# A weight transposed by TensorE in place of a DMA transpose, and another weight loaded from ScalarE's queue

## The chip, the cores and the metric

The kernel runs on one core of a Trainium2 chip. The metric is the device time of one execution in microseconds (us), measured around the whole program. The five engines of a core that matter here are PE (TensorE, the matrix unit), DVE (VectorE), ACT (ScalarE), POOL (GpSimd) and SP (SyncE, which here only issues transfers). Each takes its own instructions strictly in order, so an instruction that waits holds up everything behind it on its engine. Transfers are issued from SP, ACT or POOL and are carried by sixteen DMA engines that all of them share.

## What is computed

The reference is a transformer block with its gradient. The forward part is a pre-norm attention over a short dilated window (each token sees itself and seven earlier tokens, two apart, 32 heads of width 16), followed by a pre-norm feed-forward layer with the tanh form of gelu. Sizes: 2048 tokens, width 512, hidden width 1792, all in bf16.

```python
h  = x + attention(layernorm(x), wqkv) @ wo     # window of 8 tokens, stride 2
u  = layernorm(h) @ w1 + b1                     # [2048, 1792]
h2 = h + gelu(u) @ w2 + b2                      # first output
```

The other seven outputs are the gradients of `sum(h2 * grad_out)` with respect to x, wqkv, wo, w1, b1, w2 and b2. For the change it matters that the backward pass needs `w2` transposed: the gradient of the gelu output is `grad_out @ w2.T`.

## The kernel before

The 2048 tokens are worked on in four chunks of 512 (`NC = 4`, `CH = 512`). In a name such as `psq2_10` of the code the first digit is the chunk. Activations mostly go with tokens on the 128 partitions, or transposed with features on the partitions.

The forward pass goes through these functions, each called once for a chunk `c`. `f_ln1` normalises and transposes the input. `f_qkv(c, sel)` multiplies by one third of `wqkv` and writes the result to scratch tensors in device memory (`q_r`, `k_r`, `v_r`), from where it is read back in another layout. `f_attn` makes the logits (products on DVE, line 313, whose sums over the head width PE does with a matrix of ones, `sel`, line 320), the softmax (the exponential is line 436), and writes the weights to the scratch tensor `at_r` from POOL (line 179). `f_o` reads them back into the tile `a` (line 300, four small transfers on SP), multiplies them with `v` on DVE (line 330, tiles `pbo`), sums on PE (line 336, `pso`), copies the sums on ACT (line 451, `otm`) and transposes the result (lines 274 and 276, `pto` and `oT`). `f_h` multiplies by `wo` (line 463, `psh`), adds the input, normalises and transposes again (`ptb`, `ln2T`). `f_ffn1` is the first feed-forward product (line 506, `psf`) and gelu, which uses ACT (lines 508, 510, 518) and DVE (515, 516, 520) in turn. `f_ffn2` is the second product (line 535, `ps`) and needs `w2` as it lies in memory.

The functions are Python that emits instructions. `mix` and `take` interleave two generators by hand: `mix(f_ffn1(2), f_ffn2(1))` lets the second product of one chunk fill the first of the next. After that a scheduler places the instructions of each engine with its own estimate of when operands are ready, so the order on an engine differs from the order of the source. `gate(ins, key)` makes an instruction wait until a marked one has run: `("e", 1, 0)` is the first exponential of chunk 1, `("e", 3, 1)` the second of chunk 3, `("o", 1, 0)` the first `otm` copy of chunk 1.

PSUM tiles are taken by tag. `ptile(name, "T")` and `ptile(name, "U")` each have one buffer: 128 partitions times 1024 bf16 elements, which holds eight transposed blocks of 128 by 128. A second set of eight can start only when the first has been copied out. The tags "A", "B" and "L" have two buffers.

Weights: `w1` is loaded once as it lies, by POOL, into the slot of tag "w1", which the tiles for x of chunks 1 and 2 and the transposed ln1 of chunk 1 used before. `w2` is loaded likewise. The backward pass needs `w2T` and `w1T`; both are made by a DMA transpose on SP that reads the weight from device memory (lines 602 and 632). `w2T` takes the slot of `wqkv`, whose own transposes (`turn_w_gen`, lines 483 to 495) are made by PE before. Its first reader is the backward product at line 697 (`psg`). On SP's queue the transpose stands directly ahead of the four loads of `a` for chunk 3.

The backward pass runs over the chunks in the order 3, 0, 1, 2, first through the feed-forward layer (`b1_gg`, `b1_gx`, with `gw2_gen` between), then through attention.

Of the kernel before, what the change touches and what calls it, by code (L numbers as in the profile page):

```python
# [10 lines left out]
P = 128  # L11
BF16 = mybir.dt.bfloat16
# [23 lines left out]
def kernel(  # L36
# [20 lines left out]
    nc = tc.nc  # L57
# [5 lines left out]
    F = B_w1.shape[1]  # L63
# [3 lines left out]
    DC = D // P  # L67
    FT = F // P
# [8 lines left out]
    def pool(name, bufs, side="left", space=None):  # L77
        kw = {} if space is None else {"space": space}
        return tc.alloc_tile_pool(name=name, bufs=bufs, side=side, reuse_waits="tile", **kw)
# [15 lines left out]
    def acc(name, tag="A"):  # L95
        return psum.tile([P, CH], F32, name=name, tag=tag, bufs=1 if tag in "TU" else 2)

    def ptile(name, tag="T"):
        return psum.tile([P, 8 * P], BF16, name=name, tag=tag, bufs=1 if tag in "TU" else 2)
# [4 lines left out]
    sync, pq = nc.sync, nc.gpsimd  # L104
    mark = {}

    def behind(ins, first):
        tc.add_manual_dep(ins.ins, first.ins.name,
                          mybir.DependencyInfo(mybir.DependencyClass.Sync, mybir.DependencyReason.DATA), reason="begin later")

    def gate(ins, key):
        behind(ins, mark[key])


    ident = const.tile([P, P], BF16, name="ident")
# [41 lines left out]
    def pv(d_t):  # L157
        return d_t[:, :].rearrange("p (t d) -> p t d", t=TC)
# [26 lines left out]
    fw = pool("fw", 1, side="right")  # L185
# [14 lines left out]
    xs, w1, w2 = {}, [], []  # L200
    early1 = fl.tile([P, DC * F], BF16, name="early1", tag="w1", bufs=1)

    def load_x(c, nm="x", eng2=None):
        if nm == "x" and c in (1, 2):
            t_ = early1[:, c * TC * D:(c + 1) * TC * D].rearrange("p (j d) -> p j d", j=TC)
        else:
            t_ = get(fr, [P, TC, D], BF16, f"{nm}{c}", "x", 2)
        for ins in rows(sync, xf, c, t_, False, eng2):
            if nm == "x" and c in (1, 2):
                gate(ins, ("r", 3))  # L210
            if nm == "xr":
                gate(ins, ("o", c, 0))
        return t_
# [40 lines left out]
    def layernorm(src, dst, rstd, c, nm):  # L254
        st = const.tile([P, TC, 6], F32, name=f"st{nm}{c}", tag=f"st{nm}", bufs=2)
        mv = const.tile([P, TC, 2], F32, name=f"mv{nm}{c}", tag=f"mv{nm}", bufs=2)
        ve = const.tile([P, TC], F32, name=f"ve{nm}{c}", tag=f"ve{nm}", bufs=2)
        for j in range(TC):
            nc.vector.bn_stats(out=st[:, j, :], in_=src[:, j, :])
            nc.vector.bn_aggr(out=mv[:, j, :], in_=st[:, j, :])  # L260
        nc.vector.tensor_scalar(out=ve[:], in0=mv[:, :, 1], scalar1=EPS, scalar2=None, op0=ALU.add)
        r = rstd[:, c * TC:(c + 1) * TC]
        mark["r", c] = nc.gpsimd.tensor_tensor(out=r, in0=ve[:], in1=half[:], op=ALU.pow)
        for j in range(TC):
            nc.vector.tensor_scalar(out=dst[:, j, :], in0=src[:, j, :], scalar1=mv[:, j, 0:1],
                                    scalar2=r[:, j:j + 1], op0=ALU.subtract, op1=ALU.mult)

    def to_T(src, dst, nm, tag, tag2=None):
        for d2 in range(DC // 2):
            pt = ptile(f"pt{nm}{d2}", tag2 if tag2 and d2 else tag)  # L270
            for i in range(2):
                for j in range(TC):
                    dc = 2 * d2 + i
                    nc.tensor.transpose(pt[:, (i * TC + j) * P:(i * TC + j + 1) * P],  # L274
                                        src[:, j, dc * P:(dc + 1) * P], ident[:])
            nc.scalar.copy(out=dst[:, 2 * d2:2 * d2 + 2, :], in_=pt[:].rearrange("p (i t) -> p i t", i=2))
# [180 lines left out]
    def f_h(c):  # L457
        x, oT = load_x(c, "xr"), oTs.pop(c)
        h = fb.tile([P, TC, D], BF16, name=f"h{c}", tag="h", bufs=2)
        for j in range(TC):  # L460
            ps = acc(f"psh{c}_{j}")
            for g in range(G):
                nc.tensor.matmul(ps[:], lhsT=oT[:, g, j * P:(j + 1) * P], rhs=wo[:, g, :], start=(g == 0), stop=(g == G - 1))
            nc.vector.tensor_tensor(out=h[:, j, :], in0=ps[:], in1=x[:, j, :], op=ALU.add)
        ln2 = fr.tile([P, TC, D], BF16, name=f"ln2_{c}", tag="t1", bufs=1)
        layernorm(h, ln2, rstd2, c, "b")
        pq.dma_start(out=pv(ln2_d[c]), in_=ln2[:])
        ln2T = fl.tile([P, DC, CH], BF16, name=f"ln2T{c}", tag="ln2T", bufs=2)
        to_T(ln2, ln2T, f"b{c}", "U")
        hs[c], l2T[c] = h, ln2T  # L470
# [4 lines left out]
    def dgelu(y, u, s, t):  # L475

        nc.vector.tensor_tensor(out=y[:], in0=y[:], in1=u[:], op=ALU.mult)
        nc.scalar.activation(out=t[:], in_=s[:], func=ACT.Identity, bias=one_t[:], scale=-1.0)
        nc.vector.tensor_tensor(out=y[:], in0=y[:], in1=t[:], op=ALU.mult)
        nc.vector.tensor_scalar(out=y[:], in0=y[:], scalar1=1.0, scalar2=None, op0=ALU.add)  # L480
        nc.vector.tensor_tensor(out=y[:], in0=y[:], in1=s[:], op=ALU.mult)

    def turn_w_gen():

        for src, col, d_t in [(wqkv, sel * D, wqkv_d[sel]) for sel in range(3)] + [(wo, 0, wo_d)]:
# [8 lines left out]
            pq.dma_start(out=d_t[:, :], in_=t_[:].rearrange("p j d -> p (j d)"))  # L494
            yield

    def f_ffn1(c):
        ln2T = l2T[c]
        gts[c] = []
        for f2 in range(FT // 2):  # L500
            u = fl.tile([P, 2, CH], BF16, name=f"u{c}_{f2}", tag="u", bufs=3)
            for i in range(2):
                ft = 2 * f2 + i
                ps = acc(f"psf{c}_{ft}", "B")
                for dc in range(DC):
                    nc.tensor.matmul(ps[:], lhsT=w1[0][:, dc, ft * P:(ft + 1) * P], rhs=ln2T[:, dc, :],  # L506
                                     start=(dc == 0), stop=(dc == DC - 1))
                nc.scalar.activation(out=u[:, i, :], in_=ps[:], func=ACT.Identity, bias=b1c[:, ft:ft + 1], scale=1.0)  # L508
            z = fl.tile([P, 2, CH], BF16, name=f"z{c}_{f2}", tag="z", bufs=2)
            nc.scalar.activation(out=z[:], in_=u[:], func=ACT.Square)  # L510
            if c == 3:
                tag = "bu" if f2 < 4 else "bs"
                y = ys[f2] = br2.tile([P, 2, CH], BF16, name=f"y{c}_{f2}", tag=tag, bufs=4)
                nc.vector.tensor_scalar(out=y[:], in0=z[:], scalar1=6.0 * GC * GK, scalar2=2.0 * GC, op0=ALU.mult, op1=ALU.add)
            nc.vector.tensor_scalar(out=z[:], in0=z[:], scalar1=GK, scalar2=1.0, op0=ALU.mult, op1=ALU.add)
            nc.vector.tensor_tensor(out=z[:], in0=z[:], in1=u[:], op=ALU.mult)  # L516
            s = fl.tile([P, 2, CH], BF16, name=f"s{c}_{f2}", tag="s", bufs=2)
            nc.scalar.activation(out=s[:], in_=z[:], func=ACT.Sigmoid, scale=2.0 * GC)  # L518
            gt = fb.tile([P, 2, CH], BF16, name=f"g{c}_{f2}", tag="g", bufs=GB)
            nc.vector.tensor_tensor(out=gt[:], in0=u[:], in1=s[:], op=ALU.mult)  # L520
            gts[c].append(gt)
            if c == 3:
                dgelu(y, u, s, z)
            r0, r1 = 2 * f2 * P, (2 * f2 + 2) * P
            for dd, t_ in ((x_d[c][r0:r1, :], u), (s_d[c][r0:r1, :], s), (g_d[r0:r1, c * CH:(c + 1) * CH], gt))[2 if c == 3 else 0:]:
                pq.dma_start(out=dd.rearrange("(i p) t -> p i t", p=P), in_=t_[:])  # L526
            yield
# [14 lines left out]
    def take(gen, n=1):  # L542
        for _ in range(n):
            next(gen, None)

    def mix(gen, gen2, steps=1):
        for _ in gen:
            take(gen2, steps)
        take(gen2, 100)
# [30 lines left out]
    nc.vector.tensor_copy(out=b1c[:], in_=ptb[:, 0:FT])  # L580
    f_attn(1)
    w1.append(fl.tile([P, DC, F], BF16, name="w1", tag="w1", bufs=1))
    gate(pq.dma_start(out=w1[0][:], in_=B_w1.rearrange("(dc p) f -> p dc f", p=P)), ("e", 1, 0))
    f_o(0)
    f_h(0)
    f_qkv(2, 2)
    mix(f_ffn1(0), none)
    f_o(1)
    w2.append(fb.tile([P, FT, D], BF16, name="w2", tag="w2", bufs=1))
# [8 lines left out]
    f_h(2)  # L598
    take(turn_w, 2)
    f_attn(3)  # L600
    w2T = fw.tile([P, DC, F], BF16, name="w2T", tag="wq", bufs=1)
    gate(sync.dma_start_transpose(out=w2T[:], in_=B_w2[:, :]), ("e", 3, 1))
    mix(f_ffn1(2), f_ffn2(1))
    f_o(3)
    f_h(3)
    fr.release()
    br1 = pool("br1", 1, side="right")
    b1_order = (3, 0, 1, 2)
# [328 lines left out]
    for c in range(NC):  # L937
# [4 lines left out]
        if c == 2:  # L942
            load_otm()
            load_ln1a(bl, (0, 1, 2), ("g", 3, 0))
            for sel in range(3):
                gate(pq.dma_start(out=wqkvT[:, sel * DC:(sel + 1) * DC, :],
                                  in_=wqkv_d[sel][:, :].rearrange("p (j d) -> p j d", j=DC)), ("g", 3, 0))
# [12 lines left out]
    wg, wq, wk = gwqkv_gen(2), gwqkv_gen(0), gwqkv_gen(1)  # L960
# [54 lines left out]
```

## Time and profile before

| | before |
|---|---|
| median of 6 runs | 708.0 us (705.83 to 710.4) |
| the profiled execution, its own time | 710.08 us |
| its span from first to last instruction | 708.3 us |
| TensorE clock granted, mean | 0.96 |
| busy: PE, DVE, ACT, POOL | 89%, 78%, 56%, 30% |
| moved by DMA | 163.57 MB |
| DMA transpose of `w2`: issue on SP, until landed | 9.87 us, 16.0 us |
| load of `w1` by POOL: issue, until landed | 0.78 us, about 11.7 us |

An execution has three parts. Up to about 250 us lies the forward pass, in which PE has gaps: its busy share by ten microseconds varies between 5 and 10. From there to the end PE is busy almost without a break. Times in the timeline count from the start of the span. The letter q behind an engine's name (SPq) marks the issuing of transfers. Square brackets behind an instruction give how long the engine stood idle just before it, and what ended that.

### The profile page before, as it was taken

Reading aid. Unit: us, or ns where it says so; the run is one execution under the profiler, and the core shown is the slowest. Engines: PE = TensorE matmul, PEld = TensorE weight load, DVE = VectorE, ACT = ScalarE, POOL = GpSimd, SP = SyncE. Lnnn points to the kernel's source line nnn. Section 1 sums busy time; section 2 is a strip of 40 time slices with the busy share of each in tenths; the row PEclk is TensorE's granted clock in tenths of the full one; section 3 lists DMA queues with packets and bytes.
Section 4 is the critical chain, followed back from the end, with each engine's and each line's share of the span. In section 5 each row is a group of like instructions: output and inputs, shape, how many; then the busy total and the mean of one; then the engine's idle time right before and its main releaser. Section 6 shows DMA issues by size and latency. Waiting matters only on the chain. (4 is left out here: it accounts for less than half of the span.)

```text
span 708.3 us, 10333 instructions
## 1 busy us (share of the span) xinstructions
PE 626.9 (89%) x3682; PEld 264.6 (37%) x3682; DVE 555.8 (78%) x919; ACT 395.3 (56%) x548; POOL 209.8 (30%) x318
## 2 busy tenths in 40 slices
PE   1897668779698599999999999999999999999995
PEld 0433223234243134444444444443533333334442
DVE  5568957688973849975998788476879998999845
ACT  4654425777947739845867687551131134457553
POOL 4324433534523533452443433313200410000100
PEclk9999877979989799999999999999999999999998
DMA  8598899664889769576775985848899999996912
GB/s 219 161 267 232 204 304 364 231 235 163 257 288 228 238 159 234 173 215 227 216 207 100 227 165 151 260 108 242 311 336 350 317 346 286 333 314 195 247 59 67
DMA packets 103222, 163.57 MB, mean 231 GB/s; under 512 B 60962, under 2 KB 69251, under 8 KB 103171
## 3 DMA queue, kind: packets, MB, share of 16 engines
q1 hardware_dynamic: 73824, 78.40, 39.8%
q0 software_dynamic: 24720, 80.07, 35.2%
q10 hardware_dynamic: 4626, 4.46, 1.9%
q8 instruction: 28, 0.46, 0.3%
q14 instruction: 24, 0.19, 0.1%
HBM read 90.97 MB, written 56.71 MB: 208 GB/s over the span
## 5 line engine op out<-in xcount | busy, mean ns | idle before, releaser
L330 DVE TENSOR_TENSOR pb<-ba,r 128x2048 bf16<-128x2048 bf16 x96 | 111.2, 1215 | 1.8 <-DMA r<-k_r 1.8
L506 PE MATMUL psf<-ln2T,w 128*128 128x512 bf16 x224 | 59.8, 404 | 11.7 <-ACT u L508 11.6
L535 PE MATMUL ps<-w,g 128*128 128x512 bf16 x224 | 55.7, 379 | 0.0
L788 PE MATMUL psw<-h1tm,ln2a 128*128 128x512 bf16 (+1 forms) x256 | 54.3, 354 | 0.0
L667 PE MATMUL psw<-gout,gtm 128*128 128x512 bf16 x208 | 51.3, 379 | 2.5 <-DMA gtm<-g_d 1.7
L719 PE MATMUL psx<-w1T,gh 128*128 128x512 bf16 x216 | 50.4, 379 | 0.0
L330 DVE TENSOR_TENSOR pbo<-a,v 128x2048 bf16<-128x2048 bf16 x32 | 38.2, 1215 | 12.5 <-DMA a<-at_r 7.7
L372 ACT CAST qkv<-psq 128x512 bf16<-128x512 f32 x48 | 27.5, 586 | 30.9 <-PE psq L370 29.9
L697 PE MATMUL psg<-goutT,w2T 128*128 128x512 bf16 x168 | 42.3, 379 | 0.0
L508 ACT ACTIVATE u<-psf,b1c 128x512 bf16<-128x512 f32 x56 | 36.2, 682 | 7.8 <-PE psf L506 5.5
L313 DVE TENSOR_TENSOR pag<-go,bv 128x2048 bf16<-128x2048 bf16 x24 | 28.6, 1218 | 10.6 <-DMA go<-go_r 5.8
L506 PEld LDWEIGHTS <-w 128*128 128x128 bf16 x224 | 21.1, 101 | 41.8 <-issue 24.8
L710 POOL DMA_DIRECT2D h1tm_d<-th x27 | 20.6, 763 | 52.5 <-ACT th L708 38.2
L863 ACT ACTIVATE gt<-pss 128x512 bf16<-128x512 f32 x32 | 19.1, 598 | 29.8 <-PE pss L336 29.8
L518 ACT ACTIVATE s<-z 128x1024 bf16<-128x1024 bf16 x28 | 29.6, 1060 | 10.6 <-DVE z L516 7.1
L788 PEld LDWEIGHTS <-ln2a 128*128 128x128 bf16 x256 | 22.6, 98 | 29.2 <-issue 11.7
L708 ACT COPY th<-pth 128x1024 bf16<-128x1024 bf16 x27 | 27.0, 999 | 10.9 <-PE pth L706 8.8
L689 ACT ACTIVATE by<-bu 128x1024 bf16<-128x1024 bf16 x21 | 22.2, 1057 | 19.2 <-DVE gb1p L699 16.4
L929 PE MATMUL psq<-gt,ln1a 128*128 128x512 bf16 x128 | 32.5, 380 | 0.0
L892 PE MATMUL psy<-wqkvT,gT 128*128 128x512 bf16 x128 | 31.8, 379 | 0.2 <-DVE lua L653 0.2
L526 POOL DMA_DIRECT2D g_d<-g x28 | 20.4, 729 | 36.6 <-DVE g L520 34.5
L336 PE MATMUL pss<-pb,sel 128*32 128x512 bf16 x384 | 29.5, 384 | 1.8 <-DVE pb L330 1.7
(221 smaller groups left out, 1360.5 us busy)
## 6 DMA issues: line engine op xcount, KB each, us to landing
v<-v_r SPq DMA_DIRECT2D x16, 576.0 KB, 7.0
r<-go_r SPq DMA_DIRECT2D x16, 576.0 KB, 7.8
r<-k_r SPq DMA_DIRECT2D x16, 576.0 KB, 6.2
r<-q_r SPq DMA_DIRECT2D x16, 576.0 KB, 5.3
g_d<-g POOLq DMA_DIRECT2D x28, 256.0 KB, 4.2
h1tm_d<-th POOLq DMA_DIRECT2D x27, 256.0 KB, 4.4
h1tm<-h1tm_d POOLq DMA_DIRECT2D x3, 2048.0 KB, 12.0
x_d<-u POOLq DMA_DIRECT2D x21, 256.0 KB, 5.2
```

What stands on the lines that cost most here:

```text
L330: last = nc.vector.tensor_tensor(out=pr[:], in0=_ap(a_ap, [a_ap.ap[0], [2 * H, CJ], [0, Q4], [1, H]], off=wh * H + (4 * H * wh if sg else 0)),
L336: mm = nc.tensor.matmul(ps[PR * n:PR * n + PR, :], lhsT=sel4[:], rhs=prs[wh][:, TC * n:TC * n + TC, :, :].rearrange("p j d h -> p (j d h)" ...
L506: nc.tensor.matmul(ps[:], lhsT=w1[0][:, dc, ft * P:(ft + 1) * P], rhs=ln2T[:, dc, :], start=(dc == 0), stop=(dc == DC - 1))
L508: nc.scalar.activation(out=u[:, i, :], in_=ps[:], func=ACT.Identity, bias=b1c[:, ft:ft + 1], scale=1.0)
L518: nc.scalar.activation(out=s[:], in_=z[:], func=ACT.Sigmoid, scale=2.0 * GC)
L535: nc.tensor.matmul(ps[:], lhsT=gs[ft // 2][:, ft % 2, j * P:(j + 1) * P], rhs=w2[0][:, ft, :], start=(ft == 0), stop=False)
L667: nc.tensor.matmul(ps[:], lhsT=gtm[:, t, :], rhs=gout[t // TC][:, t % TC, :], start=(t == 0), stop=(t == NT - 1))
L697: nc.tensor.matmul(ps[:], lhsT=w2T[:, dc, ft * P:(ft + 1) * P], rhs=gT[:, dc, :], start=(dc == 0), stop=(dc == DC - 1))
L719: nc.tensor.matmul(ps[:], lhsT=t1s[ft // 2][:, ft % 2, j * P:(j + 1) * P], rhs=w1T[:, ft, :], start=(ft == 0), stop=(ft == FT - 1))
L788: nc.tensor.matmul(ps[:, 0:nf * P], lhsT=ln2a[:, t // TC, t % TC, dc * P:(dc + 1) * P], rhs=tmx[:, t, 0:nf * P], start=(t == 0), stop=(t = ...
L892: nc.tensor.matmul(ps[:], lhsT=gT[sel][:, g, j * P:(j + 1) * P], rhs=wqkvT[:, sel * G + g, :], start=(n == 0), stop=(n == NJ - 1))
L929: nc.tensor.matmul(ps[:], lhsT=ln1a[t // TC][:, t % TC, dc * P:(dc + 1) * P], rhs=gts[sel, t // TC][:, t % TC, :], start=(t == 0), stop=(t ...
```

## The change

`w2T` is no longer made by a DMA transpose. A new generator, `turn_w2_gen`, transposes the copy of `w2` that already lies in SBUF: seven steps, each of eight PE transposes of a 128 by 128 block into a PSUM tile of tag "T" and one ACT copy of 128 x 1024 elements into `w2T`. All seven steps are emitted after `f_h(3)`, and the scheduler places them from there. Second, the load of `w1` is issued by ACT's queue instead of POOL's, with the same gate.

```diff
+    def turn_w2_gen():
+
+        for k in range(FT // 2):
+            pt = ptile(f"ptw2{k}", "T")
+            for dc in range(DC):
+                for i in range(2):
+                    nc.tensor.transpose(pt[:, (2 * dc + i) * P:(2 * dc + i + 1) * P],
+                                        w2[0][:, 2 * k + i, dc * P:(dc + 1) * P], ident[:])
+            nc.scalar.copy(out=w2T[:, :, 2 * k * P:(2 * k + 2) * P], in_=pt[:].rearrange("p (dc t) -> p dc t", dc=DC))
+            yield
+
     def f_ffn1(c):
...
     w1.append(fl.tile([P, DC, F], BF16, name="w1", tag="w1", bufs=1))
-    gate(pq.dma_start(out=w1[0][:], in_=B_w1.rearrange("(dc p) f -> p dc f", p=P)), ("e", 1, 0))
+    gate(nc.scalar.dma_start(out=w1[0][:], in_=B_w1.rearrange("(dc p) f -> p dc f", p=P)), ("e", 1, 0))
...
     f_attn(3)
-    w2T = fw.tile([P, DC, F], BF16, name="w2T", tag="wq", bufs=1)
-    gate(sync.dma_start_transpose(out=w2T[:], in_=B_w2[:, :]), ("e", 3, 1))
     mix(f_ffn1(2), f_ffn2(1))
     f_o(3)
     f_h(3)
+    w2T = fw.tile([P, DC, F], BF16, name="w2T", tag="wq", bufs=1)
+    turn_w2 = turn_w2_gen()
+    take(turn_w2, 8)
     fr.release()
```

## The prediction, made before the changed kernel had run

> **What bounds the kernel now.** I read four views: the page's busy shares with a table of stretches of ten microseconds, the chain of waits that ended last, and the timelines around the two edits.
>
> Page and table of stretches (busy us of PE, PEld, DVE, ACT, POOL, then PE clock, DMA share, GB/s):
>
> ```profile
> PE 626.9 (89%) x3682; PEld 264.6 (37%) x3682; DVE 555.8 (78%) x919; ACT 395.3 (56%) x548; POOL 209.8 (30%) x318
> ```
> ```profile
> 220.00:230.00 10.00, 8.26 (x37) 3.25 (x36) 4.38 (x8) 6.21 (x8) 2.88 (x5) 1.00 0.71 214
> 230.00:240.00 10.00, 6.53 (x24) 1.94 (x23) 8.08 (x12) 7.41 (x10) 5.67 (x8) 0.66 0.62 183
> 240.00:250.00 10.00, 5.58 (x46) 2.12 (x44) 8.26 (x12) 7.83 (x11) 4.98 (x7) 0.83 0.78 275
> 250.00:260.00 10.00, 8.58 (x43) 3.57 (x44) 7.37 (x18) 0.80 (x2) 2.41 (x4) 1.00 0.36 111
> ```
>
> From about 250 on PE is dense to the end: its waits after 262 sum to about 10 us in 446. The chain that ended last covers only the last 26 us and is PE work; it says nothing of the edits. So what counts is when that dense part begins, and how much PE work is put into it. Before 250 PE has gaps, and whatever ends them moves the rest. The removed transpose lies in one such gap:
>
> ```profile
> 166.00 2.43 POOL L179 DMA_DIRECT2D at_r<-attn  x4 [3.69 <-DVE attn L440]
> 169.97 2.39 SPq L300 DMA_DIRECT2D a<-at_r  x4
> ...
> 208.59 9.87 SPq L602 DMA_TRANSPOSE w2T<-in_B_w_dram  x1
> 212.51 2.21 POOL L179 DMA_DIRECT2D at_r<-attn  x4 [1.68 <-DVE attn L440]
> 223.34 2.39 SPq L300 DMA_DIRECT2D a<-at_r  x4
> 227.86 1.23 DVE L330 TENSOR_TENSOR pbo<-a,v 128x2048 bf16<-128x2048 bf16 x1 [5.33 <-DMA a<-at_r]
> 231.79 1.06 ACT L518 ACTIVATE s<-z 128x1024 bf16<-128x1024 bf16 x1 [5.40 <-DVE z L516]
> 233.47 3.57 PE L506 MATMUL psf<-ln2T,w 128*128 128x512 bf16 x8 [5.21 <-ACT u L508]
> 237.65 1.22 DVE L330 TENSOR_TENSOR pbo<-a,v 128x2048 bf16<-128x2048 bf16 x1 [1.40 <-PE pso L336]
> ```
>
> DVE stands 5.33 us for the tile `a` of chunk 3, then ACT 5.40 for DVE, then PE 5.21 for ACT: one gap, three engines. The loads of `a` were not held by the transpose's issue, which ended at 218.46; they waited until 223.3 for the stores to `at_r`. Those landed in about 8.9 us (median of their row in this window), against 2.0 to 2.6 us in chunk 2 (first two lines), where no large transfer ran. The transpose, in flight until 224.6, slowed them.
>
> The load of `w1` lies in a like place one chunk after the start:
>
> ```profile
> 72.22 0.63 ACT L436 ACTIVATE e<-e 128x512 f32<-128x512 f32 x1 [5.76 <-DVE e L430]
> 86.83 0.78 POOL L583 DMA_DIRECT2D w<-in_B_w_dram  x1
> 93.69 5.68 SPq L300 DMA_DIRECT2D a<-at_r  x4
> 98.56 0.51 POOL L250 DMA_DIRECT2D at_r<-wqkv  x1 [4.15 <-DMA w<-in_B_w_dram]
> 102.31 1.23 DVE L330 TENSOR_TENSOR pbo<-a,v 128x2048 bf16<-128x2048 bf16 x1 [2.34 <-DMA a<-at_r]
> ```
>
> The exponential it is gated on ran at 72.22, but POOL reached the load at 86.83, behind stores that wait for DVE. It was in flight until 98.5. The stores to `at_r` of chunk 1 (issued 84.59 to 86.76) took 6.9 us, the loads of `a` behind them 5.68 us to issue in place of 2.39, and DVE waited 2.34 for them.
>
> **What the skill says.** The Trainium skill, "DMA: Bandwidth & Descriptors", section "Issuing engines are not separate DMA queues": transfers from the three issuing engines interleave on the same sixteen DMA engines, and another issuer saves only issue time. The trace agrees in the slowed stores above: POOL's stores suffer under SP's transpose. So for `w1` it is the earlier start that counts, not the queue. Same page, "Latency and other measured facts": DMA transposes reach 261 GB/s; here 1.84 MB took 16.0 us, 115 GB/s, beside other traffic, so the measurement stands. "TensorE: Matmul & The Clock Gate", "Back-to-back issue gap": N/2.4 + 2.5 ns when warm, 56 ns for 128 columns. The trace agrees: eight transposes of line 274 take 0.61 us, with one at 0.219, so (0.61 - 0.219)/7 = 0.056. Same page, Part 1: after some 3.4 us without work the array drops to half speed. The trace agrees: after the 5.21 us gap the clock reads 0.50 to 0.54, and eight matmuls of line 506 take 3.57 us in place of 1.9.
>
> **Part one, w2T.** Removed: one SP instruction and its 16 us of traffic. The stores to `at_r` (212.51 to 214.72) should then land in 2 to 3 us, by 217.5; `a` is issued till about 220 and lands as now 2.1 us after its last issue, at 222. DVE reaches the product at 222.52, the end of the `o` line ahead of it. That is 227.86 - 222.52 = 5.3 us. What is late next is PE's order: the first `ps` group (until 226.4) and `psf` pair (until 228.3) stay where they are. ACT then needs 1.3 us for two evacuations, the next `psf` pair runs warm at 228.2 to 230 (now 233.47 to 237.04), `pso` is summed at 230.4, and the fourth product can start at about 231.5 in place of 237.65. So the gap is worth 6.1, of which 0.8 is the half clock and the wait of 1.40 behind it. Bounds: 3 (stores land in 5 us as others do in busy stretches) to 7.2 (5.3 plus both later DVE idles, 1.40 and 0.52).
>
> Added: 56 PE transposes and 7 ACT copies. In the instruction order of the changed program the first group stands after the first `pso` of chunk 3, a thin place; six stand between the `psh` matmuls and the `ptb` transposes of chunk 3, where PE is dense. 6 x 8 x 0.056 = 2.7 us of PE, at no cover. Seven copies at 1.01 us (row of line 493) make 7.1 us of ACT; 9.2 us of idle ACT lie there, from 250.3 to 259.5, and 0.99 us before an `otm` copy for the first one. The chain through it: the second `psh` group waits 0.6 longer, the groups wait for the copy before them (one PSUM buffer, about 0.6 + 1.0 + handover 0.2 us a group), and the last-but-one copy stands ahead of `ln2T` on ACT. I get `ln2T` 1.3 us later against its inputs, and seven `ps` matmuls (1.5 us) left over for PE. That is 2.8, the same as the PE count. Not both: I take 2.7. If the buffer bites harder, six groups at 2.0 us are 12 us in a stretch of 10.7 (250.4 to 261.05): 1.3 us more. `w2T` is first read at 289.46 and is ready near 262, so the reader waits in no case.
>
> Part one: -6.1 + 2.7 = -3.4 us.
>
> **Part two, w1.** POOL loses one instruction of 0.78 us and the ring wait of 4.15 behind it; the zero pads for `q_r` and others move ahead, small. ACT gets the issue right behind the exponential, at 72.9. An issue on ACT is seen only for 128 KB loads, 0.45 us each; SP's 576 KB loads take 0.6. I take 1 us, between 0.5 and 2; ACT is idle from 73.8 to 78.9, so nothing waits. The load then runs from about 75 to 86. DMA share was 0.34 and 0.36 in 78 to 82, that is 2.6 us of empty DMA time, so part of it is free. Stores and loads of chunk 1 find the engines clear: `a` is there by 97. DVE reaches its product at 99.98, after the third statistics line (99.81 + 0.17), so 102.31 - 99.98 = 2.3 us. Next late are the `psh` matmuls of chunk 0, which `w1` doesn't touch. On SP one `v` load moves ahead of the input rows of `f_h(0)`, which now go at 86 in place of 84.8 and are needed at 94.6; the `k` and `q` loads of chunk 2 go behind `a`, near 96, needed at 110.
>
> Against it: ACT's new order puts the second exponential of chunk 1 ahead of two `qkv` copies, which then start at 80.4 in place of 78.9. PE's next `psq` waits for them, and `pso` comes 0.9 later, with DVE's fourth product behind it. And the loads of `a` for chunk 0, issued 69.8 to 72.2 and used at 77.94, now meet `w1`. Net -1.4, bounds -3.4 (all the empty DMA time and more) to +1.0.
>
> Sum: -3.4 - 1.4 = -4.8 against the profiled execution: span 708.3 to 703.5, its time 710.08 (1.8 more than the span) to 705.3. That execution lies 2.1 above the median, so against the median 708.0 I forecast 703.2 us. A measurement of this kernel can tell about 0.5% (3.5 us) from no change; the lines are 704.5 and 711.5.
>
> **Rivals.**
> 1. More comes free: the gap gives 7.2, the clock stays full around 106 to 118 too (0.5 there now), and `w1` gives 3.4. -7.2 + 2.7 - 3.4 = -7.9, 700.1 us. For it: three engines share the gap. Against: PE's fixed order.
> 2. The gap closes only by half, as the stores to `x_d`, `s_d` and `ln_d` alone keep the DMA engines busy: -3 + 2.7 - 1.4 = -1.7, 706.3 us. For it: 2.86 MB of POOL's traffic in those 20 us. Against: chunk 2's 2.0 to 2.6.
> 3. Slower: the single PSUM buffer. PE waits in order at each group for ACT's copy of the one before, with `psh`, `ps` and `ptb` behind it. 2.7 + 1.3, with the copies ahead of both `ln2T` copies, 2 us more: +6.0. It decides once the gap gives less than that; with a gap of 1 (stores as slow as now) and `w1` at +0.5, +5.5, 713.5 us. For it: tag "T" has one buffer and the scheduler set the groups between critical instructions. Against: 9.2 us of idle ACT.
>
> **Chances.** Forecast 0.58 (own range 701 to 705.5), rival 1 0.18, rival 2 0.13, rival 3 0.11. The range goes from 698.5, below rival 1, to 708.5, past rival 2; it leaves rival 3 out. Faster: rival 1 and about four fifths of the forecast's case, 0.18 + 0.48 = 0.66. Same: the rest of it and rival 2, 0.22. Slower 0.12.
>
> **What would show it.** Stores to `at_r` of chunk 3 landing in under 4 us; no wait of over 1 us at the first `pbo` of chunk 3; PE at clock 1.0 in the stretch after. `ptw2` groups with waits on ACT that sum to under 3 us. `w1` issued near 73 and DVE's first chunk 1 product within 0.5 us after statistics. Wrong: that wait still over 3 us; `ln2T` of chunk 3 starting over 3 us later after the last `psh` than now (259.54 after 253.67); or the product of chunk 0 at 77.94 waiting for `a`.

## The result, and the profile after

| | median us | range | runs |
|---|---|---|---|
| before | 709.31 | 705.05 to 714.89 | 73 |
| changed | 704.85 | 701.19 to 712.66 | 36 |

The ratio is 0.9941, 95% interval 0.9926 to 0.9957. On 709.3 us that is 4.2 us less, between 3.1 and 5.2. The profiled execution of the changed kernel has a span of 704.5 us, against 708.3 before. Measured again later with another group of kernels the ratio was 0.9933 (0.9911 to 0.9956). All ratios here leave out executions more than 1.5% above the fastest of the same kernel, which matters for e7_dma_later_w1_pool below, where that is seven of 22 and the quotient of the medians over all of them is 0.996.

The busy shares, from the page of the changed kernel:

```profile
PE 632.2 (90%) x3738; PEld 268.2 (38%) x3738; DVE 555.3 (79%) x919; ACT 402.5 (57%) x555; POOL 210.0 (30%) x317
```

PE has 56 instructions more and ACT 7 more: the transposes and their copies. The table of stretches of ten microseconds, of the changed kernel (start and end, the length of the stretch, then busy us of PE, PEld, DVE, ACT and POOL, then PE clock, DMA share, GB/s):

```profile
220.00:230.00 10.00, 10.00 (x51) 3.90 (x49) 9.19 (x15) 9.50 (x13) 5.50 (x8) 1.00 0.57 199
230.00:240.00 10.00, 5.46 (x52) 2.01 (x48) 10.00 (x14) 10.00 (x14) 5.86 (x9) 0.93 0.97 319
240.00:250.00 10.00, 9.40 (x70) 5.42 (x67) 6.32 (x15) 6.61 (x8) 3.23 (x5) 0.90 0.41 140
250.00:260.00 10.00, 9.21 (x64) 4.83 (x64) 3.26 (x8) 7.44 (x10) 3.72 (x7) 1.00 0.92 190
```

The first row was a gap, with DVE busy 4.38 us of ten and ACT 6.21. Now all three engines are full in it, and the clock of 0.66 in the second row is 0.93. The timeline of the changed kernel around that place, five engines together:

```profile
212.12 2.22 POOL L179 DMA_DIRECT2D at_r<-attn  x4 [1.67 <-DVE attn L440]
215.87 2.38 SPq L300 DMA_DIRECT2D a<-at_r  x4
222.04 1.22 DVE L330 TENSOR_TENSOR pbo<-a,v 128x2048 bf16<-128x2048 bf16 x1
225.97 3.70 PE L517 MATMUL psf<-ln2T,w 128*128 128x512 bf16 x16
229.60 0.61 PE L336 MATMUL pso<-pbo,sel 128*32 128x512 bf16 x8
230.34 1.22 DVE L330 TENSOR_TENSOR pbo<-a,v 128x2048 bf16<-128x2048 bf16 x1
244.38 0.61 PE L503 MATMUL ptw<-ident,w 128*128 128x128 bf16 x8
246.59 0.61 PE L503 MATMUL ptw<-ident,w 128*128 128x128 bf16 x8
251.66 1.01 ACT L505 COPY w2T<-ptw 128x1024 bf16<-128x1024 bf16 x1 [1.70 <-PE ptw L503]
252.79 1.01 ACT L276 COPY ln2T<-ptb 128x1024 bf16<-128x1024 bf16 x1
```

The stores to `at_r` are issued at the same time as before, but the loads behind them at 215.87 in place of 223.34. How long the stores took to land is in the view of DMA issues (count, size of each, median us from issue to landing; 208.5 to 231), first of the kernel before, then of the changed one:

```profile
at_r<-attn POOLq DMA_DIRECT2D x4, 64.0 KB, 8.9
at_r<-attn POOLq DMA_DIRECT2D x4, 64.0 KB, 2.0
```

The first product of chunk 3 (`pbo`) carries no wait where it had 5.33 us. Sixteen `psf` matmuls take 3.70 us where eight took 3.57. The fourth product is at 230.34 (before: 237.65). The transposes (`ptw`) show no wait in brackets: PE never stood for their one PSUM buffer. ACT's copies wait for PE, not the other way.

The second edit, in the timeline of the changed kernel (ACT's queue, SP's, and DVE):

```profile
74.41 0.41 ACTq L594 DMA_DIRECT2D w<-in_B_w_dram  x1
84.90 3.29 SPq L282 DMA_DIRECT2D v<-v_r  x2
88.31 1.92 SPq L172 DMA_DIRECT2D xr<-in_A_x_dram  x4
92.21 2.87 SPq L300 DMA_DIRECT2D a<-at_r  x4
97.25 1.29 DVE L464 TENSOR_TENSOR h<-psh,xr 128x512 bf16<-128x512 f32 x2 [5.07 <-DMA xr<-in_A_x_dram]
102.25 1.19 DVE L330 TENSOR_TENSOR pbo<-a,v 128x2048 bf16<-128x2048 bf16 x1
```

The load goes out 0.66 us after its exponential, costs ACT 0.41 us and has landed 8.2 us after its issue. The wait of 2.34 us for `a` is gone. But a few microseconds earlier DVE now stands for `xr`, the input rows of `f_h(0)`. Before, the line with these rows had ended its wait on PE:

```profile
94.64 0.69 DVE L464 TENSOR_TENSOR h<-psh,xr 128x512 bf16<-128x512 f32 x1 [4.67 <-PE psh L463]
```

The two lines can't be compared by their times, since in this execution the exponential itself came 1.53 us later (73.75 against 72.22), ahead of any edit. Single executions differ by such amounts, so below I compare stretches between two landmarks of one execution: **A** from that exponential to the first `ln2T` copy of chunk 0; **B** from the second `ln2T` copy of chunk 2 to that of chunk 3; **C** from there to the second copy into `goutT_first`, early in the backward pass.

### The profile page after: what moved, and what is told of

Its sections match the earlier page's. It is cut to its first block, busy times and chain, and to the rows that moved or that the text cites. A ratio compares the mean times of both kernels' runs of the same rounds, so it can differ in the third digit from the quotient of the medians.

```text
span 704.5 us, 10439 instructions
## 1 busy us (share of the span) xinstructions
PE 632.2 (90%) x3738; PEld 268.2 (38%) x3738; DVE 555.3 (79%) x919; ACT 402.5 (57%) x555; POOL 210.0 (30%) x317
## 5 line engine op out<-in xcount | busy, mean ns | idle before, releaser
L517 PE MATMUL psf<-ln2T,w 128*128 128x512 bf16 x224 | 57.3, 392 | 7.0 <-ACT u L519 7.0
L806 ACT CAST ow<-psw 128x512 bf16<-128x512 f32 (+1 forms) x16 | 8.5, 533 | 40.6 <-PE psw L800 34.2
```

## The experiments

My theory after the result: the first edit alone carries the gain (a gap of 6 to 7 us, less PE's transposes), and the second gains nothing because the rows take the place of `a`. The rivals: the second edit carries a good part; the transposes cost nothing, being in idle PE time; or PE's one PSUM buffer bites. The runs, with the landmark stretches of their one profile each (each ratio is to the kernel before as measured in the same group):

| run | w2T by | w1 on | rows | ratio (95%) | A | B | C |
|---|---|---|---|---|---|---|---|
| before | DMA | POOL | | 1 | 37.79 | 49.06 | 30.39 |
| changed | PE | ACT | | 0.9941 (0.9926 to 0.9957) | 36.36 | 42.86 | 31.18 |
| e1_w2t_only | PE | POOL | | 0.9951 (0.9930 to 0.9972) | 36.61 | 43.56 | 31.17 |
| e2_w1_only | DMA | ACT | | 1.0026 (1.0002 to 1.0049) | 36.30 | 50.72 | 30.38 |
| e3_dma_later | late DMA | ACT | | 0.9946 (0.9925 to 0.9966) | 35.44 | 42.43 | 30.38 |
| e4_double | PE, twice | ACT | | 0.9971 (0.9952 to 0.9990) | 37.38 | 43.36 | 33.16 |
| e5_xr_early | PE | ACT | early | 0.9886 (0.9830 to 0.9942) | 34.80 | 43.01 | 31.19 |
| e7_dma_later_w1_pool | late DMA | POOL | | 0.9925 (0.9896 to 0.9954) | 37.06 | 42.67 | 35.86 |
| e8_dma_later_xr_early | late DMA | ACT | early | 0.9894 (0.9840 to 0.9947) | 36.05 | 41.75 | 33.90 |
| e9_no_turn | none | ACT | | 0.9867 (0.9824 to 0.9910) | 37.32 | 42.09 | 30.41 |
| e10_change_again | PE | ACT | | 0.9933 (0.9911 to 0.9956) | 36.85 | 43.70 | 31.16 |
| e11_xr_early_again | PE | ACT | early | 0.9894 (0.9840 to 0.9949) | 34.79 | 42.71 | 31.17 |
| e12_xr_early_w1_pool | PE | POOL | early | 0.9969 (0.9945 to 0.9993) | 36.89 | 43.63 | 31.16 |

Four runs (e5, e8, e9, e11) have only six executions, the others 22 or more. The ratios of these four lie 0.0015 to 0.003 below the plain quotients of their medians (0.9915, 0.9922, 0.9891 and 0.9909), so a difference of that size in them is not evidence by itself.

**The two edits apart.** e1_w2t_only is the changed kernel with one line put back, e2_w1_only the kernel before with only that line:

```
-    gate(pq.dma_start(out=w1[0][:], in_=B_w1.rearrange("(dc p) f -> p dc f", p=P)), ("e", 1, 0))
+    gate(nc.scalar.dma_start(out=w1[0][:], in_=B_w1.rearrange("(dc p) f -> p dc f", p=P)), ("e", 1, 0))
```

> The transposes on TensorE alone; w1 is loaded by POOL as before. If the gain comes from the removed DMA transpose (my theory): about 3.4 us faster than before (ratio 0.995), the first product of chunk 3 on DVE no longer waits over 1 us for the tile a, and the stretch after 215 looks as in the changed kernel. If it comes from the earlier w1 load: no gain, ratio 1.000 or above.

> The w1 load on ACT's queue alone; w2T comes by DMA transpose as before. Theory: a small gain, 0 to 1.4 us (ratio 0.998 to 1.000), because the earlier arrival of a for chunk 1 is partly paid back by the input rows of chunk 0, which now stand behind a v load on SP. Rival, the w1 load carries the gain: 3 us or more, ratio 0.996 or less. Rival, it costs: ratio over 1.001.

The first edit alone gives 0.9951, 3.5 us, most of the gain. The second alone gives 1.0026: no gain, rather a small loss. With the first edit in, adding the second changes the ratio by 0.001, inside both intervals. The timeline of e2_w1_only, DVE's lines:

```profile
96.22 1.29 DVE L464 TENSOR_TENSOR h<-psh,xr 128x512 bf16<-128x512 f32 x2 [4.99 <-DMA xr<-in_A_x_dram]
...
227.38 1.23 DVE L330 TENSOR_TENSOR pbo<-a,v 128x2048 bf16<-128x2048 bf16 x1 [7.16 <-DMA a<-at_r]
```

The wait for `xr` comes with the second edit alone. The wait behind the DMA transpose is there too, longer than before (7.16 against 5.33), and stretch B with it. Why the loss reached 1.8 us by the ratio (1.3 between the medians) stays open; that wait is one candidate, seen in one execution.

**The transpose kept on DMA, but later.** In place of the PE transposes, one SP instruction behind the loads of chunk 3:

```
-    turn_w2 = turn_w2_gen()
-    take(turn_w2, 8)
+    gate(sync.dma_start_transpose(out=w2T[:], in_=B_w2[:, :]), ("o", 3, 3))
```

> As the changed kernel, but w2T comes by DMA transpose again, gated on the last otm copy of chunk 3 and behind the loads of a and of the input rows on SP. It has the gap closed and no PE transposes. Theory (the gap is worth 6 to 7 us and the transposes cost 2.7): 2 to 3 us faster than the changed kernel, 6 to 7 us faster than before, ratio about 0.990. Rival, the transposes on PE cost nothing: same as the changed kernel, 0.994. Rival, DMA traffic of a transpose hurts wherever it is, for w1T and the loads of grad_out come behind it: slower than the changed kernel, 0.996 or more.

> The kernel before with one difference: the DMA transpose of w2 is issued late, on SP behind the loads of a and of the input rows of chunk 3; w1 stays on POOL. It has no PE transposes. Theory (w1's move is worth nothing that shows): ratio 0.994 to 0.996, as in the run with the late transpose and w1 on ACT (0.9946), and the first pbo of chunk 3 doesn't wait. Rival (w1's move costs 1.8 us, as it did alone): ratio 0.991 to 0.9925.

Stretch B falls to 42.43 and 42.67: the gap closes just as well when the DMA transpose is only out of the way of the stores to `at_r`. So it was the place that cost, not the way of transposing. Moving the transpose takes away both its traffic and its slot on SP, and these runs don't separate the two. The trace of the kernel before does: the slot alone would have held the loads only until 218.46, and with 2.4 us to issue and 2.1 to land, `a` would have been there near 223.0, 0.4 after DVE was ready. That is an estimate; the rest of the 5.33 is the slow stores. But the 2 us of PE work that this saves did not show: 0.9946 and 0.9925, where I had expected about 0.990. The lower of the two lies where I had put the rival by which moving `w1` costs 1.8 us; but the intervals overlap, and the medians, 705.67 and 708.61, give 0.996, so this pair doesn't tell what moving `w1` is worth. The timeline of e7_dma_later_w1_pool, SP's queue and PE:

```profile
241.19 12.58 SPq L616 DMA_TRANSPOSE w2T<-in_B_w_dram  x1
253.89 16.51 SPq L643 DMA_TRANSPOSE w1T<-in_B_w_dram  x1
274.16 4.48 SPq L675 DMA_TRANSPOSE gtm_first<-g_d  x1
...
286.10 2.31 PE L678 MATMUL psw<-gout,gtm_first 128*128 128x512 bf16 x5 [6.16 <-DMA gtm_first<-g_d]
```

Three DMA transposes follow each other on SP, and PE waits 6.16 us for the third: stretch C is 35.86 in place of 30.39. In e8_dma_later_xr_early, with the same late transpose, the waits there are 1.63 (`gtm_first`) and 2.49 (`gout`); in the profile of e3_dma_later, the fastest execution of that run (700.25 us), PE doesn't wait for `gtm_first` and 0.92 us for `gout`. The price is paid in some executions and not in others, which fits their wide ranges (e7: 697.58 to 719.81). That the later place moves the collision to the next DMA transposes is likely; no run isolates it.

**What PE's transposes cost.** e4_double writes each block twice into the same PSUM tile: 112 transposes, 7 copies. e9_no_turn has none, and ACT copies the same amount from `w2` at the same place in its order. It leaves the transposition out, so what is computed from `w2T` is not the reference's, and it takes away the hand-over between PE and ACT as well. First e4_double, then e9_no_turn:

```
-            for dc in range(DC):
+            for dc in [d for _ in range(2) for d in range(DC)]:
```

```
-            pt = ptile(f"ptw2{k}", "T")
-            for dc in range(DC):
-                for i in range(2):
-                    nc.tensor.transpose(pt[:, (2 * dc + i) * P:(2 * dc + i + 1) * P],
-                                        w2[0][:, 2 * k + i, dc * P:(dc + 1) * P], ident[:])
-            nc.scalar.copy(out=w2T[:, :, 2 * k * P:(2 * k + 2) * P], in_=pt[:].rearrange("p (dc t) -> p dc t", dc=DC))
+            gate(nc.scalar.copy(out=w2T[:, :, 2 * k * P:(2 * k + 2) * P],
+                                in_=w2[0][:, 2 * k:2 * k + 2, :].rearrange("p a (b t) -> p (a b) t", b=2)),
+                 ("o", 3, 3 if k else 2))
```

> As the changed kernel, but each block of w2 is transposed twice into the same PSUM tile, so PE does 112 transposes in place of 56 and ACT's copies stay seven. Theory, PE is dense there and 6 of 7 groups are paid in full: 2.7 us slower than the changed kernel, ratio to before about 0.998. Rival, they fall into gaps that DVE and ACT leave: same as the changed kernel, 0.994. Rival, the single PSUM buffer's chain is what costs: 4 us or more slower, ratio 1.000.

> The changed kernel without the 56 PE transposes: ACT copies the same amount from w2 itself into w2T, at the same place in its order, so w2T holds w2's blocks untransposed and what is computed from it is not the reference's. Theory (PE transposes are paid in full, 2.1 to 2.7 us): ratio 0.990 to 0.9915. Rival (they lie in PE time that is idle anyway, and only the doubled ones cost): ratio 0.993 to 0.995.

56 more cost 0.9971 - 0.9941 = 0.003, 2.1 us (0.4 to 3.9 with both intervals); stretch C shows 33.16 - 31.18 = 2.0 of it. 56 fewer give 0.9867, lower than I had expected either way; with the intervals of 0.9867 and of the changed kernel's 0.9933 on the same chip, that bounds the cost only from below, at about 1 us. The landmarks are sharper in B and C. Stretch C is 31.16 to 31.19 in all six runs with 56 transposes, 33.16 with 112, and 30.41 with none: 0.8 us. Stretch B averages 43.2 over the same six and is 42.09 without: 1.1. So the 56 cost about 1.9 us, out of 56 x 0.056 = 3.1 counted, and they are not free. It rests on one profile without them. The three with the late DMA transpose agree in B (42.43, 42.67, 41.75); with 112, B is no longer than with 56 (43.36), and C alone grows. The timeline of e4_double, PE:

```profile
245.63 1.05 PE L503 MATMUL ptw<-ident,w 128*128 128x128 bf16 x16 [0.24 <-ACT w2T L505]
248.25 1.06 PE L503 MATMUL ptw<-ident,w 128*128 128x128 bf16 x16
```

Even with groups twice as long, the wait for the PSUM buffer is 0.24 us, once.

**The input rows.** SP works in order, and the second edit had let a `v` load that waits for DVE move ahead of the rows. In e5_xr_early the rows' gate is one that keeps them ahead of it; e11_xr_early_again is the same kernel, e12_xr_early_w1_pool has `w1` on POOL besides, and e8_dma_later_xr_early joins the early rows to the late transpose:

```
-                gate(ins, ("o", c, 0))
+                gate(ins, ("o", c, 0) if c else ("e", 1, 1))
```

> The changed kernel, with the input rows of f_h(0) gated on the second exponential of chunk 1 in place of the first otm copy of chunk 0, so that SP sends them before v_10 and v_11. Theory (the earlier w1 load gains in its stage and the rows give part of it back): DVE no longer waits for xr at the first h of chunk 0, the wait of 5.07 us then ends on PE (psh) and is 0.5 to 1 us shorter; ratio to the kernel before 0.992 to 0.9935, 0.3 to 1.3 us faster than the changed kernel. Rival (the stage's end is set elsewhere, by ACT's order and the DVE work after it): the wait goes, and the ratio stays at 0.994.

> Late DMA transpose of w2 (no PE transposes), w1 on ACT's queue, and the input rows of f_h(0) early. If PE's transposes cost what they count (2.1 us) and nothing takes their place, this is the best of all, ratio 0.989 to 0.992. If the late DMA transpose, with the one of w1 right behind it, costs about as much as PE's transposes, 0.993 to 0.995.

> The changed kernel again, as the yardstick of this group. From the first measurement: ratio 0.9941; anything from 0.992 to 0.996 agrees with it.

> The changed kernel with the input rows of f_h(0) early, again, beside the changed kernel on the same chip. Theory (the wait for the rows hid a gain of about 1.5 us, read from the landmarks of its first profile): 1 to 2 us faster than the changed kernel, ratio lower by 0.0015 to 0.003. Rival (the first ratio of 0.9886 was scatter): equal within 0.001. A ratio lower by 0.005, as first measured, would say that more than this one wait went.

> The w2T part with the input rows early, and w1 on POOL as in the kernel before. Theory (the early rows only undo what moving w1 did to them): as the w2T part alone, ratio 0.994 to 0.996, with DVE's wait at the first h of chunk 0 on PE as before. Rival (early rows help whatever w1 does): 0.992 to 0.9935, the same as with w1 on ACT's queue, and then moving w1 is worth nothing even so.

The timeline of e5_xr_early, SP's queue and DVE:

```profile
84.69 1.68 SPq L172 DMA_DIRECT2D xr<-in_A_x_dram  x3
86.60 0.55 SPq L282 DMA_DIRECT2D v<-v_r  x1
...
95.46 1.29 DVE L464 TENSOR_TENSOR h<-psh,xr 128x512 bf16<-128x512 f32 x2 [3.51 <-PE psh L463]
100.47 1.19 DVE L330 TENSOR_TENSOR pbo<-a,v 128x2048 bf16<-128x2048 bf16 x1
```

The wait is shorter and ends on PE again, and the first product of chunk 1 comes 26.96 us after the exponential, against 28.50 in the changed kernel. Stretch A falls by 1.6 to 34.80, and by 2.1 in the second pair (34.79 against 36.85). A scatters, though: in the six profiles with `w1` on ACT and late rows it is 35.44 to 37.38 (mean 36.6), and e8_dma_later_xr_early, with early rows and a PE wait of 4.67, has 36.05, more than e3_dma_later without them. The ratios point the same way: 0.9886 and 0.9894 against 0.9941 and 0.9933, with overlapping intervals; the medians of the second pair, measured in one group, are 701.81 and 703.14. Both ratios fell by more than I had expected; with six executions each I read nothing from that. With `w1` on POOL the early rows bring nothing (A 36.89, ratio 0.9969, a little above the range expected), and DVE's wait there is what it was before:

```profile
96.43 0.69 DVE L464 TENSOR_TENSOR h<-psh,xr 128x512 bf16<-128x512 f32 x1 [4.67 <-PE psh L463]
```

So neither the earlier `w1` nor the earlier rows show a gain alone: stretch A is 37.1 with `w1` on POOL (mean of four profiles, 36.61 to 37.79), 36.6 with `w1` on ACT and late rows, which this scatter can't tell from 37.1, and 35.2 with both (mean of three). e5_xr_early has the lowest ratio of the versions that leave nothing out: 702.6 and 701.81 us in its two groups, beside 708.61 and 708.29 of the kernel before. That it beats the changed kernel is likely, by the wait, the means of the stretch and the medians, but not settled. In e8_dma_later_xr_early, with 0.9894, what PE saved in stretch B went into the waits for `gtm_first` and `gout` told above: C is 33.90.

## Why the prediction was right, step by step

The forecast was -4.8 us; measured were -4.2. The parts fared differently.

- **The stores and loads of chunk 3:** right. The stores landed in 2.0 us in place of 8.9, `a` was there ahead of the first product, and that ran at 222.04 without a wait. The transpose in that place was the cause: e3_dma_later and e7_dma_later_w1_pool move it without PE's help and close the same gap.
- **The gap of 6.1:** right in kind, a little small. The fourth product came 7.3 us earlier, of which 0.4 were there already ahead of the gap (the `o` line at 221.44 in place of 221.84), so 6.9. The first `psf` pair stayed where it was, as forecast; the second followed it without a pause, with ACT, no longer held up by DVE, emptying the PSUM tiles in time. What I had too large is the last step: I put 1.1 us between the `pso` sum and the fourth product without a reason, and in the trace it is 0.1 (230.21 to 230.34). One sign failed: PE's clock in the stretch after was to be 1.0 and was 0.93 and 0.90.
- **PE's transposes, 2.7:** right that they are paid, too high in size. About 1.9 by the landmarks, 2.1 by e4_double. I counted six of seven groups in full, at no cover. Of the 0.8 us that don't show, 0.35 had cover: without transposes PE waits that long for `h` ahead of the last eight `psh` matmuls (in the kernel before and in e9_no_turn), and in the changed kernel that wait is gone. The rest is not settled: PE's waits there for `oT` and `ln` (0.56 and 0.78 us in the changed kernel, 0.47 and 0.68 without transposes) are no shorter with them. The `ln2T` copies, forecast 1.3 us late against their inputs, lost about 0.6: the lead over before was 7.3 at the fourth product, and 6.75 and 6.6 at the copies, and e9_no_turn gains 1.1 at most.
- **Part one, -3.4:** e1_w2t_only measured -3.5. The two size errors make it 6.9 - 1.9 = 5.0 locally, so the hit is in part luck: some 1.5 us of it are not there in the medians. The lead was 5.8 at the `goutT_first` copy in the profiles of before and changed, 6.6 around 480, 3.8 at the end; single executions scatter by as much, and where it goes stays open.
- **Part two, -1.4:** this is the term that failed. It rests on the sentence that one `v` load moves ahead of the input rows, "which now go at 86 in place of 84.8 and are needed at 94.6". The load that moved ahead waits for DVE on SP, the `v` line takes 3.29 us, and the rows went at 88.31; DVE stood for them until 97.25. Against the exponential that is 14.56 us in place of 12.57. I priced the moved load by its issue and left out its wait. In its place the runs show no gain from the part: 1.0026 alone, 0.001 on top of the first edit. The other steps of the part were near the forecast: `w1` was issued at 74.41, ACT's issue took 0.41 (forecast 1, bounds from 0.5), `a` was no longer waited for, and ACT's changed order delayed the second `oT` copy by 0.7 (forecast 0.9). With the rows ahead of the `v` load again, `w1` and rows together bring 1.9 in the mean of stretch A. So the total came near the forecast by part one, and because part two was small.
- **The rivals:** the single PSUM buffer (713.5 us) did not bite: no wait on it in the changed kernel, 0.24 us with doubled groups. Nor did the gap close only by half. Rival 1 was right about the gap (6.9 of its 7.2) and wrong about `w1`.

## What to carry to other kernels

Here a DMA transpose cost most where it met small stores that someone was waiting for. Look at the landing times of the stores beside such a transfer, and try to move it before replacing it, minding what stands behind it in its queue. When a step is moved and a scheduler reorders a queue, look for waiting instructions that now stand ahead of a load, and price the load by the wait ahead of it, not by the issue. Where executions scatter by more than the effect, compare stretches between landmarks of one execution, and see first how far each stretch scatters between profiles of the same code: stretch C, which agreed within 0.03 over six profiles, told 0.8 us; stretch A, which scattered by 1.9, could not tell 0.5.

## What was not expected

- With the transpose of `w2` directly ahead of it on SP, the one of `w1` took 20.6 to 25.1 us to land (three profiles); in the ten others it took 15.5 to 19.6. The small one behind it, `gtm_first`, took between 1.43 and 4.48 us to issue, and that doesn't follow the order: 4.11 in e1_w2t_only, where the transpose of `w1` alone went ahead and PE didn't wait for `gtm_first`. What sets it stays open.
- The load of 1.8 MB took 8.2 us to land in the changed kernel's profile and 11.4 from POOL (not the 11.7 of the table of the kernel before), but that is scatter: in the nine profiles with the load on ACT it is 8.2 to 12.2, the 12.2 in the same kernel measured again, and in the four on POOL 10.7 to 11.4. In the prediction I cited the Trainium skill, "DMA: Bandwidth & Descriptors", section "Issuing engines are not separate DMA queues", which says that transfers run on the same sixteen DMA engines whichever engine starts them, so that another issuer saves only issue time. These landing times agree with that.
